# Constant products on TensorE between the squares of an RWKV-7 kernel's first chunk

## The chip, the cores and the metric

The kernel runs on one core of one Trainium2 chip. The metric is the device time of one execution in microseconds (us); three runs of the kernel before gave 713.66, 718.1 and 712.8, so the median is 713.66 us. The profile is one execution recorded by the hardware profiler. The engines are TensorE (PE, with its weight loads as PEld), VectorE (DVE), ScalarE (ACT) and GpSimd (POOL); SyncE (SP) issues most transfers, each engine has its own queue of instructions, and works through it in order.

## The reference

The kernel computes a linear-attention recurrence and then an MLP, all in 32-bit floats. For each of 4 x 8 batch and head pairs, over 768 steps, with a state of 40 x 40:

```
for t in range(S):
    y[:, :, t] = einsum('bhd,bhde->bhe', rt, state)
    Sa = einsum('bhde,bhe->bhd', state, at)
    state = state * wt[:, :, None, :] - einsum('bhd,bhe->bhde', Sa, bt)
    state = state + einsum('bhd,bhe->bhde', vt, kt)
x = y.transpose(0, 2, 1, 3).reshape(B * S, H * D)      # 3072 x 320
h = x @ w_in                                           # 320 x 2048, given as 64-bit floats
out = (0.5 * h * (1 + erf(h / sqrt(2)))) @ w_out       # 2048 x 320, given as 64-bit floats
```

## The kernel before

The 768 steps are cut into 12 chunks of 64. Within a chunk the recurrence is written as matrices. N (a against scaled b), A (a against scaled k), RV (r against v) and M are products of 64 x 64 blocks, masked to their strict upper triangle by VectorE (`masked`, line 575). The chunk needs the inverse of a triangular matrix made from N. Its 32 x 32 diagonal blocks are inverted first; `corner` and `joined` put the 64 x 64 inverse Tt together from them. Then follow sa and saT, M, and QY, which gives the chunk's output rows and its next state; `outputs` scales these. The MLP of a chunk is cut into pieces, and `fill` puts them between the steps of later chunks.

Chunks after the first have their 32 x 32 blocks inverted on GpSimd, column by column (`start_inverse`, lines 672 and 674), and the result goes through memory (`store_inverse`, `fetch_inverse`). The first chunk does it on TensorE (`squares`, line 712): in five rounds the power of N is squared and the inverse T is updated. A round is 64 small products, then a copy of the power by ScalarE (line 736), a transpose by VectorE (line 737) and, but for the first round, an addition to T by VectorE (line 739). The next round waits for all of these. `squares` is a generator: each `next(zero)` in the main part runs one round, and the first one only the preparation. `corner_direct` and `joined_direct` (products J and J2) then build Tt of the first chunk, with copies by ScalarE and VectorE.

Meanwhile the weights, which come as 64-bit floats, are converted by integer and float steps on VectorE, ScalarE and POOL (`to_float`, lines 319 to 333); `convert(n)` starts n such conversions and finishes those that it finds half done, and `first_load` and `second_load` bring the raw words.

The order of the work is written out by hand: `manual_schedule` keeps the instructions of each engine in the order in which the program calls for them. Waits follow from data and from buffers. All results of TensorE go to one pool of four buffers, `duo`, each of 2 x 512 columns and 128 partitions. Two helpers issue products whose result nothing uses: `warm(columns, ...)` takes a buffer of its own and multiplies the identity with a broadcast of the constant `cum_m`, one product for each argument, of 128 columns for each unit; `keep(n)` asks that the next `duo` begins with one such product of n x 128 columns, in the buffer that it hands out. Before the change `warm` is not called after its definition.

`make_y2(0)` takes the two buffers of QY. For the first chunk there is no earlier state, so it issues nothing else.

Of the kernel before, what the change touches and what calls it, by code (L numbers as in the profile page):

```python
# [19 lines left out]
def kernel(  # L20
# [71 lines left out]
    def keep(columns):  # L92

        asked[:] = [columns]

    def duo(name):
        pt = psum.tile([P, 2, 512], FP32, tag="duo", name=name)
        while asked:
            n = asked.pop()
            mm(pt[:, 0, :n * P], ident, cum_m.unsqueeze(1).to_broadcast([P, n, P]))  # L100
        return pt

    def half(j, n=HP):
        return slice(j * HP, j * HP + n)
# [4 lines left out]
    def mm(o, lhsT, rhs, first=True):  # L109
        nc.tensor.matmul(o, lhsT, rhs, start=first, stop=True, skip_group_check=True)  # L110
# [39 lines left out]
    def rows(t):  # L150
        return t[:, :G * DM].rearrange("p (g h d) -> p g h d", g=G, h=H)
# [142 lines left out]
    def flat(t):  # L294
        return t.rearrange("p j g n t -> p (j g n) t")
# [42 lines left out]
    def convert(n, last=False):  # L338

        for _ in range(n):  # L340
            begun.append(queue.pop(0))
            next(begun[-1], None)
            if len(begun) > 1:
                next(begun.pop(0), None)
        if last:
            while begun:
                next(begun.pop(0), None)
# [62 lines left out]
    def first_pieces(kts, part, eng):  # L410
        queue.extend(first_convert(kt, part, eng) for kt in kts)
# [4 lines left out]
    def run(steps):  # L416
        for _ in steps:
            pass
# [4 lines left out]
    def logs(c):  # L423
        logw = raws[c, "w"][:, :G * DM]
        nc.scalar.activation(logw, logw, ACT.Ln)
# [66 lines left out]
    def scale_k(c, eng=nc.gpsimd):  # L492
        rwv, _ = decays[c]
        ks = turned_in[c]["ks"] = padded[:, 2 + c % 2] if c < NB else k_rows[c % 2]
        to = ks[:, :, :, :D] if c < NB else rows(ks)
        eng.tensor_tensor(to, raws.pop((c, "k")), rwv, ALU.mult)
# [35 lines left out]
    def turn_k(c):  # L532
        t = turned_in[c]
        if c >= NB:
            kT = by_batch(side("k_turned", "conv", 2))
            turn(kT, c, "k_turned")
            en = t.pop("en")
            nc.vector.tensor_tensor(en, kT, en, ALU.mult)
            t["kT"] = parts_by_batch(en)
            return  # L540
        kT = side("kT", "kT", 1)
        nc.scalar.copy(kT, flip(by_pair(t["ks"]), "kT_ps"))
        t["kT"] = parts(kT)
# [15 lines left out]
    def turn_r(c):  # L559
        rT = side("rT", "rT", 2)  # L560
        if c < NT:
            raw = raws.pop((c, "r"))
            nc.scalar.copy(rT, flip(lambda q, m: raw[:, NP * q + m].rearrange("p g d -> p (g d)"), "rT_ps"))
        else:
            turn(rT.rearrange("p q m (e t) -> p (q m e) t", e=2), c, "r")
        turned_in[c]["rT"] = parts(rT)
# [7 lines left out]
    def masked(to, pt):  # L574
        nc.vector.tensor_tensor(to, pt, upper.unsqueeze(1).to_broadcast([P, 2 * G * NP, C]), ALU.mult)  # L575

    def products(name, lT, rT, swap):

        pt = duo(name).rearrange("p j (g n t) -> p j g n t", g=G, n=NP)
        for g in range(G):  # L580
            for n in range(NP):
                for e in range(2):
                    for j in range(2):
                        mm(pt[half(e ^ j if swap else e), j, g, n], lT[half(j, D), g, n, e],
                           rT[half(j, D), g, n, e])
        return flat(pt)
# [32 lines left out]
    def make_RV(c, mask=True):  # L619
        t = turned_in[c]  # L620
        t["RV_ps"] = products("RV_ps", t["vT"], t["rT"], False)
        if mask:
            mask_RV(c)

    def mask_RV(c):
        t = turned_in[c]
        masked(flat(t["VR"])[:, :, D:], t.pop("RV_ps"))
# [12 lines left out]
    def make_av(c):  # L640
        t = turned_in[c]
        av = duo("av")[:, :, :G * NP * D].rearrange("p x (g i d) -> p x g i d", g=G, i=NP)
        for g, i, x, e, q, m in units():
            mm(av[half(e ^ x), x, g, i], t["A"][half(e), x, g, i], t["VR"][half(e), g, q, m, :D])
        avs = t["avs"] = avs_ring()
        nc.scalar.copy(avs[:, :, :DM], av.rearrange("p x g i d -> p x (g i d)"))
# [65 lines left out]
    def squares(c, turned, Z, ZT, eng):  # L712

        N = flat(turned_in[c]["N"])
        turned = turned.rearrange("p (n t) -> p n t", n=NBL)
        both = Z.rearrange("p (n x t) -> p n x t", n=NBL, x=2)
        ZT = ZT.rearrange("p (n t) -> p n t", n=NBL)
        power, T = both[:, :, 0], both[:, :, 1]
        nc.vector.transpose(turned, N)
        for rows, cols in quads:  # L720
            eng.tensor_tensor(T[rows], N[rows, :, cols], ident[rows, rows].unsqueeze(1).to_broadcast([BL, NBL, BL]),
                              ALU.add)
        yield
        for k in range(5):
            last = k == 4
            pt = duo("sq").rearrange("p z (n t) -> p (z n) t", t=2 * BL)
            for n in range(NBL):
                for rows, cols in quads:
                    if k == 0:
                        mm(pt[rows, n, :BL], turned[rows, n, cols], N[rows, n, cols])  # L730
                    elif last:
                        mm(pt[rows, n, BL:], ZT[rows, n], T[rows, n])
                    else:
                        mm(pt[rows, n], ZT[rows, n], both[rows, n].rearrange("p x t -> p (x t)"))
            if not last:
                nc.scalar.copy(power, pt[:, :, :BL])
                nc.vector.transpose(ZT, pt[:, :, :BL])
            if k:
                nc.vector.tensor_tensor(T, T, pt[:, :, BL:], ALU.add)
            yield  # L740
        nc.vector.transpose(ZT, T)
        inverses[c] = T, ZT, power

    def corner_direct(c, engs):
        T, L, Js = inverses[c]
        N = flat(turned_in[c]["N"])
        Tt = inverses[c] = Tt_ring()
        turned_in[c]["blocks"] = T, Js
        J = duo("J").rearrange("p z (n t) -> p z n t", n=NBL)
        for n in range(NBL):  # L750
            for q in range(2):
                mm(J[hi[q], q, n], N[lo[q], n, BL:], L[lo[q], n])
        for q in range(2):
            nc.scalar.copy(Js[hi[q]], J[hi[q], q])
        for (rows, cols), eng in zip(quads, engs):
            copy = eng.copy if eng is nc.scalar else eng.tensor_copy
            copy(flat(Tt)[rows, :, cols], T[rows])
# [88 lines left out]
    def make_M(c):  # L846
        t = turned_in[c]
        masked(flat(t["SM"])[:, :, D:], products("M_ps", t["saT"], t["rT"], False))

    def make_y2(c):  # L850


        t = turned_in[c]
        t["QY"] = [duo("QY")[:, :, :NP * VC].rearrange("p e (i c) -> p e i c", i=NP) for g in range(G)]
        if state[0] is None:
            return
        tn = state[0][1]
        for i in range(NP):
            for e in range(2):
                for x in range(2):  # L860
                    for g in range(G):
                        mm(t["QY"][g][half(x), e, i, D:], tn[half(g, D), e, i, half(x)],
                           t["rT"][half(g, D), i // NA, 2 * (i % NA) + x, e], i == 0)
# [189 lines left out]
    def warm(*columns):  # L1053

        pt = duo("warm")
        for n, cols in enumerate(columns):
            mm(pt[:, n % 2, :cols * P], ident, cum_m.unsqueeze(1).to_broadcast([P, cols, P]))
# [16 lines left out]
    scale_a(0)  # L1074
    make_N(0)
    zero = squares(0, spare_w, *spare_N, nc.gpsimd)
    next(zero)
    sums(1)
# [18 lines left out]
    mask_A(0)  # L1097
    turn_r(0)
    next(zero)
    next(zero)  # L1100
    make_RV(0, False)
    run(zero)
    scale_k(1, nc.vector)
    corner_direct(0, (nc.scalar, nc.scalar, nc.scalar, nc.scalar))
    first_load(False, 1, eng=nc.sync)
    make_av(0)
    make_y2(0)
    turn_k(1)
    make_X(0)
    first_pieces((1, 2), 0, nc.gpsimd)  # L1110
    mask_RV(0)
    first_pieces((3,), 0, nc.vector)
    load_VR(1)
    joined_direct(0)
# [9 lines left out]
    make_saT(0)  # L1124
    convert(0, True)
    convert(1)
    make_M(0)
    logs(2)
    keep(1)
    make_QY(0)  # L1130
    first_load(False, 2, early(5, 4), eng=nc.sync)
    convert(1)
# [235 lines left out]
```

## Time and profile before

| what | value |
|---|---|
| median of three runs | 713.66 us |
| span of the profiled execution | 709.1 us |
| median less that span | 4.6 us |
| TensorE busy | 669.7 us, 94% of the span |
| VectorE busy | 365.5 us, 52% |
| ScalarE busy | 222.3 us, 31% |
| POOL busy | 350.2 us, 49% |
| mean granted clock of TensorE | 0.958 |

The profiled execution's own time is its span and some 4.6 us around it, if it was an execution like the median one. The page also gives the busy share in 40 slices of the span, some 17.7 us each, in tenths, and under them the clock that TensorE was granted, where 9 stands for 90% or more of full speed. The same numbers can be asked for any window. The timeline lists instructions in order with their start, their duration, and in brackets the idle time before them with what ended it. In it a 32-bit product of TensorE shows as two records.

### The profile page before, as it was taken

The numbers are of one execution on the slowest core, as the hardware profiler recorded it, in microseconds if no ns is written. First come the engines' busy times: TensorE is split into PE (matmuls) and PEld (weight loads), VectorE is DVE, ScalarE is ACT, GpSimd is POOL, SyncE is SP. The second block draws the span as 40 slices with busy tenths as digits, with TensorE's granted clock in tenths as the row PEclk, the third lists the DMA queues.
The fourth block names the chain that finished last, engine by engine and source line by source line (L and its number), as shares of the span: only waits on it lengthen the run. The fifth ranks groups of instructions, "written<-read, shape, count | busy, mean of one in ns | idle before, by whom it ended". The sixth has DMA issues, their size and how long they took to land.

```text
span 709.1 us, 32732 instructions
## 1 busy us (share of the span) xinstructions
PE 669.7 (94%) x14778; PEld 587.1 (83%) x14778; DVE 365.5 (52%) x481; ACT 222.3 (31%) x308; POOL 350.2 (49%) x798
## 2 busy tenths in 40 slices
PE   7578897879999999999999999999999999999997
PEld 4567786757877877899899898998998898998987
DVE  2334689993354365375484483573671772522303
ACT  5124674444140240351241332232323413112020
POOL 5284458810851851861862853845836827800000
PEclk9775798999999999999999999999999999999999
DMA  9689538864667647656656747657648646020100
GB/s 130 121 167 151 104 87 203 136 128 88 123 122 113 132 94 110 133 100 113 124 102 121 137 87 128 125 93 128 133 84 144 130 86 85 20 55 4 31 8 19
DMA packets 287923, 74.46 MB, mean 105 GB/s; under 512 B 265736, under 2 KB 284456, under 8 KB 287784
## 3 DMA queue, kind: packets, MB, share of 16 engines
q1 hardware_dynamic: 283360, 68.20, 52.6%
q0 software_dynamic: 864, 2.36, 2.2%
q8 instruction: 116, 1.90, 1.2%
q10 hardware_dynamic: 3560, 1.80, 1.0%
q14 instruction: 23, 0.19, 0.1%
HBM read 58.69 MB, written 9.70 MB: 96 GB/s over the span
## 4 chain that ended last, share of the span: by engine, by line
PE 81%; DVE 6%; DMA 3%; ACT 3%; SPq 3%; issue 2%; ACTq 1%; DVEq 0%
PE ph L993 26%; PE po L946 19%; PE po L1010 7%; PE QY L110 6%; PE J L110 2%; PE av L110 2%; PE A_ps L110 2%; PE X L110 2%; PE sq L110 2%; PE RV_ps L110 2%; DMA a_pairs<-in_a_dram 2%; PE sap L110 2%; PE saT_ps L110 2%; PE M_ps L110 2%; PE wT_ps L110 1%
## 5 line engine op out<-in xcount | busy, mean ns | idle before, releaser
L993 PE MATMUL ph<-xt,w_in_sb 64*128 64x256 f32 x1920 | 219.4, 381 | 0.0
L672 POOL TENSOR_TENSOR tmp<-W,Nb 128x126 f32<-128x126 f32 (+22 forms) x310 | 124.3, 401 | 160.0 <-DMA Nb<-N 137.0
L993 PEld LDWEIGHTS ph<-xt,w_in_sb 64*128 64x128 f32 x1920 | 182.4, 187 | 22.1 <-issue 0.3
L674 POOL TENSOR_TENSOR W<-W,tmp 128x126 f32<-128x126 f32 (+22 forms) x310 | 132.4, 427 | 24.3
L995 ACT ACTIVATE gt<-ph 128x1024 f32<-128x1024 f32 x48 | 49.1, 1024 | 152.5 <-PE ph L993 152.3
L946 PE MATMUL po<-w_out_sb,gt 128*128 128x160 f32 x576 | 83.0, 302 | 0.1
L946 PEld LDWEIGHTS po<-w_out_sb,gt 128*128 128x128 f32 x576 | 78.7, 190 | 2.2 <-DVE gt L966 0.4
L1010 PE MATMUL po<-w_out_sb,gt 128*128 128x320 f32 x192 | 55.8, 448 | 1.1 <-ACT wpT L443 1.1
L1010 PEld LDWEIGHTS po<-w_out_sb,gt 128*128 128x128 f32 x192 | 36.7, 195 | 16.7 <-issue 1.5
L186 DVE STREAM_TRANSPOSE aT<-a_pairs 128x1024 f32<-128x1024 f32 x9 | 11.2, 1247 | 46.6 <-DMA a_pairs<-in_a_dram 46.6
L802 DVE COPY Tt<-J 32x512 f32<-32x512 f32 x9 | 6.2, 689 | 54.5 <-ACT Tt L802 54.5
L786 ACT COPY Js<-J 128x256 f32<-128x256 f32 x11 | 4.1, 370 | 94.6 <-PE J L110 94.6
L998 DVE TENSOR_TENSOR half<-gt 128x1024 f32<-128x1024 f32 x9 | 11.4, 1271 | 29.6 <-ACT gt L995 29.6
L946 PE MATMUL po<-extra,half 128*128 128x160 f32 x176 | 26.1, 303 | 0.0
L320 ACT ACTIVATE conv<-conv,rebias 128x320 uint32<-128x320 uint32 (+1 forms) x26 | 16.1, 624 | 29.0 <-DVE conv L319 23.1
L575 DVE TENSOR_TENSOR SM<-M_ps,upper 128x1024 f32<-128x1024 f32 x12 | 14.5, 1207 | 19.7 <-PE M_ps L110 19.7
L946 PEld LDWEIGHTS po<-extra,half 128*128 128x128 f32 x176 | 24.2, 190 | 0.3
L995 ACT ACT_TABLE_LOAD x10 | 12.8, 1283 | 36.0 <-PE ph L993 36.0
L950 DVE TENSOR_TENSOR os<-os,po 128x160 f32<-128x160 f32 x36 | 11.5, 319 | 23.6 <-PE po L946 17.9
L946 PE MATMUL po<-extra,gt 128*128 128x160 f32 x144 | 21.0, 299 | 0.0
L662 POOL MEMSET W<- 128x512 f32 x10 | 5.3, 528 | 31.5 <-DMA inv<-W 31.5
L886 DVE TENSOR_TENSOR xt<-QY,wpT 128x512 f32<-128x512 f32 x24 | 15.4, 684 | 10.2 <-PE QY L110 9.6
(224 smaller groups left out, 1134.7 us busy)
## 6 DMA issues: line engine op xcount, KB each, us to landing
Nb<-N SPq DMA_DIRECT2D x20, 256.0 KB
VR<-in_v_dram SPq DMA_DIRECT2D x24, 160.0 KB
out_dram<-os SPq DMA_DIRECT2D x48, 80.0 KB
b_rows<-in_b_dram SPq DMA_DIRECT2D x22, 160.0 KB
k_rows<-in_k_dram SPq DMA_DIRECT2D x22, 160.0 KB
N<-N SPq DMA_DIRECT2D x44, 64.0 KB
Tt<-inv SPq DMA_DIRECT2D x44, 64.0 KB
a_pairs<-in_a_dram SPq DMA_DIRECT2D x18, 144.0 KB
```

The source lines that it names most:

```text
L110: nc.tensor.matmul(o, lhsT, rhs, start=first, stop=True, skip_group_check=True)
L320: nc.scalar.activation(power, power, ACT.Relu, bias=rebias, scale=8.0)
L575: nc.vector.tensor_tensor(to, pt, upper.unsqueeze(1).to_broadcast([P, 2 * G * NP, C]), ALU.mult)
L672: eng.tensor_tensor(t, W[:, :rows, j:j + 1].to_broadcast([P, rows, rest]), Nb[:, j:j + 1, j + 1:].to_broadcast([P, rows, rest]), ALU.mult)
L674: eng.tensor_tensor(W[:, :rows, j + 1:], W[:, :rows, j + 1:], t, ALU.add)
L886: nc.vector.tensor_tensor(xt[:, :NP, g * P:(g + 1) * P].rearrange("p i (e t) -> p i e t", e=2), Y, wp[:, g, :, :, :C], ALU.mult)
L946: nc.tensor.matmul(po[:, n, :DM // 2], l_[:, f], r_[:, f], start=f == 0, stop=f == NF // 2 - 1)
L950: nc.vector.tensor_tensor(to, one_, other, ALU.add)
L993: nc.tensor.matmul(ph[:, x, s], w_in_sb[half(x), kt, p * P:(p + 1) * P], xt[half(x), kt], start=kt == 0, stop=kt == NK - 1)
L995: nc.scalar.activation(gt[:, 4 * q:4 * q + 4].rearrange("p (x s) t -> p x s t", x=2), ph, ACT.Gelu)
L998: nc.vector.tensor_tensor(s1, block(1, 0), block(1, 1), ALU.add)
L1010: nc.tensor.matmul(po[:, g], gt[:, f, g * P:(g + 1) * P], w_out_sb[:, f], start=f == 0, stop=f == NF - 1)
```

## The change

Eight calls of `warm` are put in. Five stand at the head of the five rounds of squares, with 2, 3, 4, 2 and 2 products of 512 columns. One with 3 follows the last round, one with 2 stands in front of `make_M(0)` and one with 2 in front of `make_QY(0)`. RV is multiplied between the last two rounds instead of after the last, and its mask follows the last round at once. `make_y2(0)` goes from behind `make_av(0)` to just in front of `make_QY(0)`, and the `keep(1)` there, whose product goes in front of the next result, vT of chunk 1, is dropped.

```
         for k in range(5):
             last = k == 4
+            warm(*(4,) * (2, 3, 4, 2, 2)[k])
             pt = duo("sq").rearrange("p z (n t) -> p (z n) t", t=2 * BL)
...
     next(zero)
+    make_RV(0, False)
     next(zero)
-    make_RV(0, False)
     run(zero)
+    mask_RV(0)
+    warm(4, 4, 4)
     scale_k(1, nc.vector)
     corner_direct(0, (nc.scalar, nc.scalar, nc.scalar, nc.scalar))
     first_load(False, 1, eng=nc.sync)
     make_av(0)
-    make_y2(0)
     turn_k(1)
     make_X(0)
     first_pieces((1, 2), 0, nc.gpsimd)
-    mask_RV(0)
     first_pieces((3,), 0, nc.vector)
...
     convert(1)
+    warm(4, 4)
     make_M(0)
     logs(2)
-    keep(1)
+    warm(4, 4)
+    make_y2(0)
     make_QY(0)
```

On TensorE the order after the change is: N of chunk 1, 2 constant products, round 1, 3 products, round 2, 4 products, round 3, kT, A, vT, rT, 2 products, round 4, RV, 2 products, round 5, 3 products, J, av, kT of chunk 1, J2, A of chunk 1, sa, saT, 2 products, M, 2 products, QY. On VectorE the mask of RV stands ahead of the scaling of chunk 1's k instead of behind it. The queues of ScalarE, POOL and SP keep their order.

More of the change, by code (lines that the diff above doesn't have):

```diff
@@ L725, in squares @@
             last = k == 4
+            warm(*(4,) * (2, 3, 4, 2, 2)[k])
             pt = duo("sq").rearrange("p z (n t) -> p (z n) t", t=2 * BL)
@@ L1099 @@
     next(zero)
+    make_RV(0, False)
     next(zero)
-    make_RV(0, False)
     run(zero)
+    mask_RV(0)
+    warm(4, 4, 4)
     scale_k(1, nc.vector)
@@ L1106 @@
     make_av(0)
-    make_y2(0)
     turn_k(1)
@@ L1110 @@
     first_pieces((1, 2), 0, nc.gpsimd)
-    mask_RV(0)
     first_pieces((3,), 0, nc.vector)
@@ L1126 @@
     convert(1)
+    warm(4, 4)
     make_M(0)
     logs(2)
-    keep(1)
+    warm(4, 4)
+    make_y2(0)
     make_QY(0)
```

## The prediction

> **What bounds the kernel now.** I read the page's forty slices first (17.7 us each), because what the change adds is work for TensorE.
>
> ```profile
> span 709.1 us, 32732 instructions
> ...
> PE   7578897879999999999999999999999999999997
> ...
> PEclk9775798999999999999999999999999999999999
> ```
>
> From slice 10 (160 us) to the end TensorE is full at full clock, so time won or lost at the start is kept only if it still stands there. All edits lie in slices 2 to 5, where TensorE is neither full nor fast. The next view is the table of windows. In windows of one us from 20 to 95 us the clock changed only near 25.5, 32.3, 35.8, 39.2, 49.4 and 80.1 us, always a multiple of 3.4 us apart; so I cut the windows there.
>
> ```profile
> 22.10:25.50 3.40, 2.01 (x111) 1.61 (x110) 0.94 (x2) 1.01 (x1) 1.54 (x1) 1.00 0.59 85
> 25.50:28.90 3.40, 1.39 (x85) 1.25 (x84) 1.00 (x2) 0.58 (x1) 0.77 (x3) 0.51 0.39 61
> 28.90:32.30 3.40, 2.97 (x113) 3.00 (x117) 0.28 (x1) 0.00 (x0) 0.00 (x0) 0.50 0.26 52
> 32.30:35.80 3.50, 1.33 (x89) 1.20 (x82) 1.29 (x2) 0.58 (x1) 0.00 (x0) 0.99 0.89 236
> 35.80:39.20 3.40, 3.40 (x87) 3.23 (x77) 0.68 (x2) 0.59 (x1) 2.56 (x10) 0.50 1.13 215
> 39.20:42.60 3.40, 2.30 (x83) 1.99 (x83) 1.35 (x3) 1.01 (x1) 2.77 (x9) 1.00 0.55 128
> ...
> 46.00:49.40 3.40, 1.23 (x104) 1.07 (x92) 1.29 (x2) 0.58 (x1) 2.93 (x7) 1.00 1.23 203
> 49.40:52.80 3.40, 2.98 (x138) 2.63 (x128) 1.62 (x3) 0.00 (x0) 2.85 (x8) 0.51 0.81 114
> ...
> 76.70:80.10 3.40, 3.40 (x81) 3.15 (x73) 1.37 (x4) 0.70 (x2) 2.55 (x2) 0.50 1.06 213
> ```
>
> The first number after the length is TensorE's busy time; the third from the end is its clock. Windows with 1.23 and 1.33 us of work were followed by half clock. After 46.0 to 49.4 it stays at 0.50 for nine windows, to 80.1; windows busy for 2.98 us of small products did not bring it back. The chain of waits says that TensorE is on the path there (squares, J, av, A_ps, sap, M_ps, QY), with Scalar and Vector steps between. These Vector steps I read from the timeline:
>
> ```profile
> 63.13 0.69 DVE L768 COPY Tt<-J 32x512 f32<-32x512 f32 x1 [7.72 <-ACT Tt L768]
> ...
> 67.19 0.82 DVE L831 COPY SM<-sap 128x640 f32<-128x640 f32 x1
> 67.94 1.21 DVE L575 TENSOR_TENSOR A<-A_ps,upper 128x1024 f32<-128x1024 f32 x1
> ...
> 71.50 0.69 DVE L324 SCALAR_TENSOR_TENSOR conv<-w_out_sb,conv 128x512 uint32<-128x512 uint32 x1 [1.68 <-ACT conv L320]
> 72.92 1.23 DVE L575 TENSOR_TENSOR SM<-M_ps,upper 128x1024 f32<-128x1024 f32 x1 [0.73 <-PE M_ps L110]
> 74.06 1.50 DVE L319 TENSOR_SCALAR conv<-w_out_sb 128x512 uint32<-128x512 uint32 x1
> ...
> 81.74 0.70 DVE L772 STREAM_TRANSPOSE L<-Tt 128x512 f32<-128x512 f32 x1
> ```
>
> VectorE is nearly closed from 63.1 to 69.8: a faster TensorE cannot pull that stretch forward.
>
> **The price of one product.** Eight 320-column products of the MLP (16 records) take 4.50 us at full clock, so 512 columns cost 4.50 / 8 x 512 / 320 = 0.90 us, and 1.8 at half. The 20 added are 18.0 us of TensorE at full clock. None waits for anything not long done, so each starts as TensorE comes free; what exceeds the old wait delays the next square.
>
> **The squares, step by step, at full clock.** A 64-column square costs 2.0 us at full clock (1.99 at 44.65) against 3.43 at half (29.33); a 32-column one 1.7 (43 records in 0.57).
> - N_ps of chunk 1 ends at 24.77, unchanged. Two products 1.8, first square 1.7: end 28.3 (before 27.82, with half clock and a 1.14 us gap called issue). I let the long products hide that gap; its bounds are 0 and 1.14.
> - Three products 2.7 in a wait of 1.5, square 2.0: 33.0 (32.80).
> - Four, 3.6, in a wait of 2.1, square 2.0: 38.6 (37.81).
> - kT now 1.06 instead of 1.74, ScalarE's copy 1.01, A_ps 1.16, vT 1.9, rT 1.0: 44.9 (44.72).
> - Two, 1.8, where there was no wait at all, square 2.0: 48.7 (46.70).
> - RV 1.16, at no cost: it lies in the 2.1 us that the last square waits for Scalar and Vector, and the copy of rT that it needs ended at 45.77. Two products 1.8 more end after that wait; last square 1.7: 53.4 (51.08).
> - Three, 2.7, against 1.5 us of Vector; J 1.04 instead of 1.92, and RV's 3.1 us (51.0 to 54.1) no longer ahead of it: **57.1 (55.96)**.
>
> So J ends 1.1 us later, although nothing runs at half clock. RV's mask (1.22) now goes ahead of the scaling of k (0.78) on VectorE. It ends near 56.8, before kT of chunk 1 wants it at 58.3; if that cover went, it would cost up to 1.2.
>
> **From J to chunk 1.** ScalarE then copies without a break: 4.46 us for Js, Tt and av, 1.01 for kT, 0.57 for Tt. Before, 1.0 us of waits for TensorE lay between. The 1.1 and the 1.0 cancel: VectorE's copy of Tt ends at 63.95 (63.82), and its closed stretch at 69.9. TensorE's part is early: sap and saT end at 66.2 (69.75), so ScalarE's conversion no longer queues behind saT's copies; the 1.68 us idle at 71.50 shrinks to 0.4, and the mask of M (whose 2 products and M itself end by 69.2) ends at 72.3 (74.15), 1.9 early. QY takes 3.0 instead of 5.83: 75.4 (80.02). Its two products lie under the mask. Taking QY's buffers later moves no instruction, as the first chunk has none there; dropping the 128-column product saves 0.3 behind QY.
>
> What is late next is L of chunk 1. Its buffer comes free with POOL's second conversion, 80.20 before. That follows ScalarE's and VectorE's conversions. The 1.50 us of L319 (0.42 elsewhere) ended just after POOL's first conversion, so I let it follow POOL: 74.5 (75.56), 1.1 early, and POOL's second ends at 79.1. L then starts at 79.1 (81.74): **2.6 early**. Bounds: 1.1, if only POOL's shift counts, to 4.6, QY's shift. L's data, stored and fetched through SP's queue, do not shift (issued to 72.9); that landing is not shown, and I take it to be before 79.
>
> TensorE waits from 77 to 80 for it, a window as thin as the ones that fell. Then J and a keep product run at half until 83.5; that returns 0 to 1.0 us, and I take 0.6. **Sum: 2.0 us less.** From there to 112 us the chain is Scalar and Vector work in order, which moves as a whole; transfers have room (DMA share 0.2 to 0.5 from 84 to 112). The profiled span of 709.1 becomes 707.1; the median of 713.66 lies 4.6 above the span, and I add that: 711.7.
>
> **A rule against the change.** Clock rows first: half clock from 35.8 follows a window whose longest wait is 2.17 us. The Trainium skill, "TensorE: Matmul & The Clock Gate", section "HAM oscillation — how this bites in real kernels", asks only that no idle gap exceed about 3.4 us. By it alone the filled waits were harmless, and the change is its 1.1 us at J: 714.8. The trace disagrees with it; I go by the rows.
>
> **Rivals.**
> 1. Overfilled waits, slower: products where there was 0 to 2.1 us of wait cost more than the clock returns. Place: the window from 25.5 and the one from 42.6. If half clock still holds in both (the windows before them are not full: 2.3 us busy with the kT wait), 1.7 us are lost in each, and J ends 4.5 late. It decides once J is more than 3.7 late, for then L is not early. With a fallen clock at 80: 1.0 + 0.8 = about 2 slower, 715.7. For it: 2.01 us busy was followed by half clock at 25.5. Against: dense products replace the small ones, and 2.30 held at 39.2.
> 2. Hidden anyway: J's delay and the closed Vector stretch eat the gain, or a later dip (the clock fell to 0.50 for 116 to 120) moves the other way: 713.7, within 1.
> 3. L isn't held by POOL: all of QY's 4.6 comes through, 709.1.
>
> **How the numbers follow.** Forecast (1 to 4 us less) 0.5, rival 1 0.2, rival 2 0.18, rival 3 0.12. The range runs from 706.5 (rival 3 and a lucky later window of 2.6) to 717.0 (rival 1 with 1.3 more of half clock). Within 1%, 7.1 us, is about what a measurement of this kernel can tell from no change; nearly all lies there. Beyond, either way, takes something that no row shows: 0.06 each.
>
> **What would show it.** Clock 1.00 from 25.5 to about 63; J ending near 57; the Vector copy of Tt unmoved near 64; M's mask 2 early; L near 79. The forecast is wrong if L319 keeps its time whatever POOL does, if half clock returns between the squares, or if the chain after 112 us does not move with L.

## The result and the profile after

The kernel after takes 718.82 us (median of nine runs, 717.06 to 722.65), the kernel before 714.0 us (nine runs on the same chip, 711.18 to 718.1). The ratio is 1.0068, with a 95% interval of 1.0043 to 1.0094: slower by some 4.8 us, where 2.0 us less was forecast. The profiled execution of the kernel after has a span of 717.1 us and a mean granted clock of 0.979 (0.958 before). That run took 718.82 us, so 1.7 us lie around the span.

The page of the kernel after: its span, TensorE's busy time with the number of its matrix instructions, the 40 slices (17.9 us each) of TensorE and of its clock, and the queue that brings the instructions.

```profile
span 717.1 us, 32807 instructions
...
PE 680.9 (95%) x14816; PEld 584.5 (82%) x14816; DVE 365.9 (51%) x481; ACT 222.2 (31%) x308; POOL 348.0 (49%) x798
...
PE   7898897869999999999999999999999999999997
...
PEclk8799999989999999999999999999999999999999
...
q8 instruction: 116, 1.90, 1.2%
```

The clock did what was hoped. In slices 3 to 5 it reads 9 throughout, where the kernel before had 7, 5 and 7, and the digits of TensorE are as high or higher in slices 2 to 5. Over 24.5 to 82.0 us the mean clock rose from 0.64 to 0.88 and TensorE's busy time from 44.27 to 49.86 us. The time is longer nevertheless. The last line, which the prediction did not use, matters below: 116 packets with 1.90 MB of instructions, 16 KB each.

The table of windows of the kernel after, cut as before (the first number after the length is TensorE's busy time, the third from the end its clock).

```profile
22.10:25.50 3.40, 1.48 (x24) 1.28 (x28) 1.75 (x2) 1.01 (x1) 1.54 (x1) 0.83 0.50 86
25.50:28.90 3.40, 3.40 (x63) 2.25 (x56) 1.23 (x1) 0.00 (x0) 0.00 (x0) 0.50 0.00 0
...
35.80:39.20 3.40, 3.40 (x94) 2.11 (x83) 1.29 (x2) 0.58 (x1) 1.81 (x7) 1.00 1.06 227
...
49.40:52.80 3.40, 3.40 (x160) 2.48 (x162) 0.00 (x0) 0.69 (x2) 2.91 (x7) 1.00 1.17 147
52.80:56.20 3.40, 1.72 (x49) 1.44 (x42) 1.29 (x2) 0.32 (x1) 2.85 (x8) 0.83 0.54 86
56.20:59.60 3.40, 3.40 (x69) 1.31 (x67) 0.00 (x0) 0.00 (x0) 2.84 (x8) 0.66 0.95 137
```

The half clock from 35.8 and the long one from 49.4 are gone. The one from 25.5 stayed, and a new, shorter one begins in the window from 52.8 and goes on into the next. That window is busy for only 1.72 us, although no engine kept TensorE waiting in it. The timeline of TensorE in the kernel after shows why (start, duration, operation; in brackets the idle time before it, and what ended it).

```profile
27.00 3.78 PE L110 MATMUL warm<-cum_m,ident 128*128 128x512 f32 x4
30.71 1.61 PE L110 MATMUL sq<-N,st 32*32 32x32 f32 x128
...
50.42 1.99 PE L110 MATMUL sq<-Nb,W 32*32 32x64 f32 x128
52.34 0.79 PE L110 MATMUL RV_ps<-rT,vT 40*64 40x64 f32 x34
54.81 0.94 PE L110 MATMUL RV_ps<-rT,vT 40*64 40x64 f32 x30 [1.68 <-issue]
55.68 3.36 PE L110 MATMUL warm<-cum_m,ident 128*128 128x512 f32 x4
58.97 1.43 PE L110 MATMUL sq<-Nb,W 32*32 32x32 f32 x128
...
63.10 1.20 PE L110 MATMUL J<-W,N 32*32 32x32 f32 x64
...
78.77 1.23 PE L110 MATMUL M_ps<-rT,saT 40*64 40x64 f32 x64
```

After 34 records of RV, TensorE stands still for 1.68 us with "issue" as the reason, which means that nothing the profile shows held it. The clock falls, and the two products behind it take 3.36 us instead of 1.8. In front of the first square the two products take 3.78 us, since the clock was half there too. ScalarE begins to copy J at 64.40 us (56.06 before), and VectorE follows:

```profile
70.26 0.69 DVE L769 COPY Tt<-J 32x512 f32<-32x512 f32 x1 [6.26 <-ACT Tt L769]
...
80.06 1.23 DVE L575 TENSOR_TENSOR SM<-M_ps,upper 128x1024 f32<-128x1024 f32 x1 [2.04 <-PE M_ps L110]
81.20 0.42 DVE L319 TENSOR_SCALAR conv<-w_out_sb 128x512 uint32<-128x512 uint32 x1
...
86.82 0.70 DVE L773 STREAM_TRANSPOSE L<-Tt 128x512 f32<-128x512 f32 x1
```

That is VectorE's timeline of the kernel after. The copy of Tt begins 7.1 us later than before (63.13), the mask of M 7.1 (72.92), L of chunk 1 5.1 (81.74). From there to the end of the span it is 630.3 us, 627.4 in the first profile of before and 630.1 in a second one that is told of below.

### The profile page after: what moved, and what is told of

Same layout as the page of the kernel before. It is cut to its first block, busy times and chain, and to the rows that moved or that the text cites. A ratio compares the mean times of both kernels' runs of the same rounds, so it can differ in the third digit from the quotient of the medians.

```text
span 717.1 us, 32807 instructions
## 1 busy us (share of the span) xinstructions
PE 680.9 (95%) x14816; PEld 584.5 (82%) x14816; DVE 365.9 (51%) x481; ACT 222.2 (31%) x308; POOL 348.0 (49%) x798
## 4 chain that ended last, share of the span: by engine, by line
PE 77%; DVE 3%; SPq 2%; ACT 2%; issue 1%; DMA 1%; ACTq 1%; DVEq 0%
PE ph L994 29%; PE po L947 19%; PE po L1011 7%; PE QY L110 6%; PE J L110 2%; PE X L110 2%; PE av L110 1%; PE sap L110 1%; PE saT_ps L110 1%; PE A_ps L110 1%; PE RV_ps L110 1%; PE M_ps L110 1%; PE N_ps L110 1%; SPq L898 1%; PE wT_ps L110 1%
## 5 line engine op out<-in xcount | busy, mean ns | idle before, releaser
L672 POOL TENSOR_TENSOR tmp<-W,Nb 128x126 f32<-128x126 f32 (+22 forms) x310 | 121.3, 391 | 159.4 <-DMA Nb<-N 136.4
L1011 PEld LDWEIGHTS po<-w_out_sb,gt 128*128 128x128 f32 x192 | 37.0, 197 | 18.1 <-ACT wpT L443 2.5
L186 DVE STREAM_TRANSPOSE aT<-a_pairs 128x1024 f32<-128x1024 f32 x9 | 11.2, 1246 | 42.3 <-DMA a_pairs<-in_a_dram 42.3
L951 DVE TENSOR_TENSOR os<-os,po 128x160 f32<-128x160 f32 x36 | 11.5, 319 | 28.9 <-PE po L947 23.2
L320 ACT ACTIVATE conv<-conv,rebias 128x320 uint32<-128x320 uint32 (+1 forms) x26 | 16.1, 623 | 29.7 <-DVE conv L319 23.3
L110 PE MATMUL warm<-cum_m,ident 128*128 128x512 f32 x40 | 23.8, 736 | 0.0
L662 POOL MEMSET W<- 128x512 f32 x10 | 5.3, 529 | 35.8 <-DMA inv<-W 35.8
```

Source lines behind the costliest of these rows:

```text
L186: nc.vector.transpose(to.rearrange("p n (s y) -> p n y s", y=2), raws.pop((c, n)).rearrange("p n (y d) -> p n y d", y=2)[:, :, :, :BL])
L320: nc.scalar.activation(power, power, ACT.Relu, bias=rebias, scale=8.0)
L672: eng.tensor_tensor(t, W[:, :rows, j:j + 1].to_broadcast([P, rows, rest]), Nb[:, j:j + 1, j + 1:].to_broadcast([P, rows, rest]), ALU.mult)
L951: nc.vector.tensor_tensor(to, one_, other, ALU.add)
L1011: nc.tensor.matmul(po[:, g], gt[:, f, g * P:(g + 1) * P], w_out_sb[:, f], start=f == 0, stop=f == NF - 1)
```

## The experiments

In what follows N is the end of chunk 1's N on TensorE, J the start of ScalarE's first copy of J, L the start of VectorE's first transposes for L. One profile is one execution, and such landmarks move: the kernel before, profiled a second time, has J at 59.26 instead of 56.06. The verdicts therefore rest on the timed ratios, and the profiles on what recurs in several.

Several theories were tried against each other, and the expectations name them by letters or by what they say. The overfilled waits are theory A: only TensorE's time counts, and a product delays the next step by what it exceeds the wait. Theory B puts the time on the new order or on QY's late buffers. Another let the loads on SP's queue hold something up. Theory F, which came last, says that TensorE also has to be fed: its instructions arrive in packets of 256, which is 128 matrix records with their 128 weight loads, and small products use these up faster than the next packet comes.

### Order, squares and tail apart

`e1_order_only` is the kernel after without any of the 20 products: the new order alone.

```
-            warm(*(4,) * (2, 3, 4, 2, 2)[k])
...
-    warm(4, 4, 4)
...
-    warm(4, 4)
     make_M(0)
     logs(2)
-    warm(4, 4)
```

> The changed kernel without any of its 20 products: RV between the last two rounds, its mask early, QY's buffers late, the keep product gone. Theory A (the products are longer than the waits that they fill): the slowdown goes; RV's 3.1 us no longer stand between the last square and J, so J ends 1 to 3 us earlier than before and the time is 711 to 714. Theory B (the new order or QY's late buffers cost the time): at least 3 of the 4.8 us stay, 717 or more.

Measured: 716.41 us against 715.22; ratio 1.0017, interval 0.9983 to 1.0051. The new order costs or brings nothing that can be told from zero, so theory B's 717 us or more did not come; the 711 to 714 us that theory A gave didn't either. In its one profile (an execution of 720.62 us) TensorE stands still with "issue" for 3.08 us in RV, which now follows the fourth square, and for 2.94 us in the fifth square: in that execution what the order was to save went there.

`e2_squares_only` is the kernel before with the products of the rounds alone.

```
         for k in range(5):
             last = k == 4
+            warm(*(4,) * (2, 3, 4, 2, 2)[k])
```

> The kernel before with only the 13 products at the heads of the five rounds; RV, its mask, QY's buffers and the keep product as before. Theory A: 13 products of 0.9 us are 11.7 at full clock, and the waits of the rounds hold 1.5 + 2.1 + 2.1 of them, so J ends 6 to 9 us late, and with half clock for some of the products more; part of it comes back by full clock after J: 716 to 721. Theory B: within 1 us of before, 713 to 715.

Measured: 724.17 us, ratio 1.0109 (1.0074 to 1.0145). The products of the rounds are slower by themselves, and seem to cost more than the whole change (1.0068), though the two intervals overlap.

`e3_tail_only` is the kernel after without that line; the three products behind the rounds, those in front of M and QY, and the order stay.

> The changed kernel without the 13 products of the rounds, but with the new order and with the 3 + 2 + 2 products behind the last round and in front of M and QY. Theory A: J ends at most 2 us later than before (2.7 of products in a wait of 1.5, RV no longer there), and the 3 us that the changed kernel won between J and L of chunk 1 stay: 709 to 713. Theory B: 717 or more. Third theory (without products in the rounds the clock falls before J and what follows J wins nothing): 713 to 716.

Measured: 719.44 us, ratio 1.0049 (1.0015 to 1.0082). That is slower where theory A gave 709 to 713 us, though only three of its products stand between N and J; its profile is of a quick execution (716.0 us), and what makes its median long stays open. The parts don't add up (1.0109 and 1.0049 against 1.0068 for both): the one gives back a part of what the other costs.

`without_M_QY` tries one part. It is the kernel after without the four products in front of M and QY.

```
-    warm(4, 4)
     make_M(0)
     logs(2)
-    warm(4, 4)
     make_y2(0)
```

> The changed kernel without the four products in front of M and QY. In its profile M's products started 2.4 us after the last copy of saT (76.37 to 78.77) because two products at half clock stood before it, and QY 0.5 after its mask. Theory A: M's mask ends 1.5 to 2.5 us earlier after J, L 1.5 to 2.5 earlier, time 716 to 717.5. If full clock for QY is what these four buy: QY takes 5 us instead of 3.2, the two cancel, 718 to 719.5.

Measured: 721.59 us against 714.93; ratio 1.0098 (1.0063 to 1.0132). Its timeline of TensorE has M and QY at half clock again:

```profile
77.67 2.46 PE L110 MATMUL M_ps<-rT,saT 40*64 40x64 f32 x64 [0.69 <-ACT saT L843]
81.46 3.05 PE L110 MATMUL QY<-SM,extra 64*64 64x104 f32 x64 [1.33 <-DVE SM L575]
```

From J to L it takes 24.7 us, the two profiles of the kernel before 25.7 and 24.0, and three of the kernel after 22.4, 22.6 and 22.2. Over all runs, eight profiles without these four products have 23.3 to 25.7 us and eight with them 21.3 to 23.2; `e4_fit`, told of next, has two of the four and 25.8. So the four products in front of M and QY return some 2.5 us from J to L, and the loss lies between N and J. The timed ratios agree in sign, but their intervals overlap.

### Fewer and more products

`e4_fit` sizes the products to the waits of the kernel before: 0, 1, 2, 0 and 1 in the rounds, 1 behind them, 1 in front of M and 1 in front of QY.

```
-            warm(*(4,) * (2, 3, 4, 2, 2)[k])
+            warm(*((), (4,), (4, 4), (), (4,))[k]) if k in (1, 2, 4) else None
...
-    warm(4, 4, 4)
+    warm(4)
...
-    warm(4, 4)
+    warm(4)
     make_M(0)
     logs(2)
-    warm(4, 4)
+    warm(4)
```

> The changed kernel with fewer products, sized to the waits at full clock: none, 1, 2, none and 1 at the heads of the rounds, 1 behind the last, 1 in front of M and 1 in front of QY, 7 instead of 20. Theory A: no wait is overfilled by more than 0.3 us at full clock, so J ends at 54 to 57, the win after J stays, 707 to 711. Theory B: 717 or more. If the clock cannot be held with 7 products: 711 to 715.

Measured: 716.83 us, ratio 1.001 (0.9976 to 1.0044): like the kernel before. The 707 to 711 us of theory A did not come.

`no_wait_places` leaves out the products of rounds 1 and 4, where the kernel before had no wait.

```
-            warm(*(4,) * (2, 3, 4, 2, 2)[k])
+            if k in (1, 2, 4):
+                warm(*(4,) * (2, 3, 4, 2, 2)[k])
```

> The changed kernel without the two products of round 1 and the two of round 4, the places where the square had no wait at all; 16 products stay. Theory A (products beyond a wait are paid in full): J ends 3 to 4 us earlier after N than with all 20 (33 to 34.5 us instead of 37.3), and the time is 714 to 716. Theory F (the packets set the pace, and the products lie under their lateness): the gaps come back where the products were, J moves by less than 1.5 us, the time stays at 717 to 719.

Measured: 717.6 us, ratio 1.0036 (1.0005 to 1.0068). That is about half the loss, as far as overlapping intervals tell.

`two_waits_only` is the kernel before with one product in the wait of round 2 and two in that of round 3.

```
+            if k in (1, 2):
+                warm(*(4,) * k)
```

> The kernel before with three products alone: one of 0.9 us in the 1.5 us wait of round 2, two of 1.8 in the 2.1 us wait of round 3; nothing else moves. Theory A: none is beyond its wait, the squares of rounds 2 and 3 run at full clock and save up to 2.3 us: 712.5 to 715. Theory F or a full clock that is worth nothing here: kT, the packets and ScalarE's copies take the gain back, 714.5 to 717.

Measured: 716.06 us, ratio 1.002 (0.9993 to 1.0047). Even products that fit a real wait bring nothing that can be told from zero.

`double_dose` is the kernel after with 4, 6, 8, 4 and 4 products in the rounds, 13 more, which are 11.7 us of TensorE at 0.90 each.

> The changed kernel with twice the products in the rounds: 4, 6, 8, 4 and 4, that is 13 more, 11.7 us at full clock. Theory A (the waits are already overfilled): every added product delays J in full, J ends 10 to 13 us later than 64.4 less the 2 to 3 us of half clock that denser work avoids, and the time is 727 to 731. Theory F (packets set the time; products only lie under their lateness): part of the added time hides the packets, J ends 5 to 8 later, 722 to 726.

Measured: 722.33 us against 715.28; ratio 1.0121 (1.0076 to 1.0166). Its profile (an execution of 728.15 us, the slowest of four) has the clock at 1.00 from 7.1 to 75.3 us:

```profile
7.10:75.30 68.20, 59.23 (x1489) 39.26 (x1488) 18.33 (x22) 21.08 (x27) 31.47 (x76) 1.00 0.84 138
```

Its timeline of TensorE has a stop before J, and another behind it:

```profile
67.44 0.25 PE L110 MATMUL J<-W,N 32*32 32x32 f32 x3 [0.28 <-issue]
...
72.15 0.37 PE L110 MATMUL J<-Nb 32*32 32x32 f32 x11 [1.41 <-issue]
```

Here the aim of the change is fully met, and the kernel is slower still. But 11.7 us more of products lengthened N to J by only 4.5 us and the time by some 3.5: something else was hidden under them. That is in the range of theory F and not in that of theory A.

### Where the time between N and J goes

The timelines of TensorE, added up from N to J: constant products, waits for another engine (the bracket names one), stops with "issue", and the rest, which is the useful products.

| run | N to J | products | waits | issue | rest |
|---|---|---|---|---|---|
| before | 31.3 | 0 | 7.0 | 2.4 | 21.9 |
| before_again | 35.0 | 0 | 7.0 | 4.7 | 23.4 |
| after | 37.3 | 18.0 | 1.1 | 1.7 | 16.6 |
| after_again | 40.7 | 16.5 | 1.1 | 5.0 | 18.0 |
| after_control | 38.9 | 18.4 | 1.1 | 2.2 | 17.1 |
| double_dose | 43.5 | 26.0 | 1.1 | 0.3 | 16.1 |
| e1_order_only | 38.1 | 0 | 6.4 | 8.4 | 23.2 |
| e2_squares_only | 39.0 | 12.1 | 1.4 | 5.4 | 20.1 |
| e3_tail_only | 36.7 | 4.1 | 4.8 | 5.8 | 22.0 |
| e4_fit | 36.2 | 7.8 | 1.4 | 5.8 | 21.2 |
| no_wait_places | 37.8 | 14.7 | 1.1 | 4.3 | 17.7 |
| without_M_QY | 39.4 | 14.8 | 1.1 | 4.3 | 19.2 |
| two_waits_only | 32.5 | 4.0 | 3.5 | 3.4 | 21.5 |
| quiet_before | 33.7 | 0 | 7.0 | 5.0 | 21.8 |
| quiet_after | 38.7 | 14.8 | 1.1 | 4.7 | 18.1 |
| dense_products | 49.6 | 16.3 | 1.1 | 11.2 | 21.1 |
| before_small | 38.0 | 1.6 | 4.8 | 7.6 | 24.1 |

Means of the two profiles of before and the three of after: the products cost 17.6 us; they bring back 5.9 of waits, 5.4 in the useful products by the faster clock, and 0.6 of stops. That leaves 5.8 us lost from N to J (33.2 to 38.9; the parts are rounded). With the 2.5 us returned from J to L the loss is 3.3 us, less than the timed 4.8. These parts are rough: the four profiles without products between N and J have 31.3 to 38.1 us (mean 34.5), the five with all sixteen 37.3 to 40.7 (mean 39.0), which makes the loss there 4.5 us. Where the rest of the timed 4.8 lies the profiles don't show. L itself is 4.9 later in these profiles, because N, ahead of every edit, was 1.5 later in them, by chance as far as the runs show (24.1 to 27.1 over all of them, with no tie to the edits).

`before_again` and `after_again` are second profiles of the two kernels, with one time each.

> The kernel before, unchanged, profiled a second time. In all traces so far TensorE stands still at every 128th small product (records 984, 1112, 1239 of its stream) and goes on 1.3 to 1.7 us after a 16 KB packet of the instruction queue has landed. Theory F (the time of the first chunk is set by how late these packets come, which changes from execution to execution): the gaps before records 984, 1112 and 1239 differ from the first profile's 0.41, 0.84 and 0.66 us by 1 to 3 us in sum, J ends at 57 to 62 instead of 55.96, the span is 711 to 716. Theory A alone (only the products matter): J ends within 1 us of 55.96 and the span within 2 of 709.1.

> The changed kernel, unchanged, profiled a second time. Its first profile began the edited stretch late (N of chunk 1 ended at 27.07, not 24.2 to 25.8 as in the eight other traces) and with half clock. If that was one execution's bad luck: N ends at 24.2 to 25.8, J 36 to 38 us after it (37.3 in the first profile), so at 60 to 63, L 22 to 23 us after J, span 713 to 718. If the products themselves cause it: N ends at 27 and J at 64 again.

Measured: 715.14 us with a span of 713.4, and 720.43 us with a span of 718.7. So 1.7 us lie around a span, and the first profile of the kernel before was a quick execution. The timeline of TensorE in `before_again`:

```profile
25.75 1.39 PE L110 MATMUL sq<-N,st 32*32 32x32 f32 x85 [0.74 <-issue]
...
51.99 1.18 PE L110 MATMUL sq<-Nb,W 32*32 32x32 f32 x72 [2.01 <-issue]
53.10 1.77 PE L110 MATMUL RV_ps<-rT,vT 40*64 40x64 f32 x56
56.82 0.49 PE L110 MATMUL RV_ps<-rT,vT 40*64 40x64 f32 x8 [1.94 <-issue]
57.24 1.92 PE L110 MATMUL J<-W,N 32*32 32x32 f32 x64
```

In the first profile of the kernel before:

```profile
26.41 1.39 PE L110 MATMUL sq<-N,st 32*32 32x32 f32 x85 [1.14 <-issue]
...
49.90 1.19 PE L110 MATMUL sq<-Nb,W 32*32 32x32 f32 x72 [0.41 <-issue]
...
53.62 0.49 PE L110 MATMUL RV_ps<-rT,vT 40*64 40x64 f32 x8 [0.84 <-issue]
```

The stops stand at the same places of the program in both: in front of the last 85 records of the first square, the last 72 of the fifth, the last 8 of RV. Only their length changes. Counted through the stream of matrix records they are 128 apart, give or take two (in the first profile records 984, 1112, 1239, 1366 and 1494), and when an edit adds records they shift by just as many: RV stops after 56 records in the kernel before, after 34 in the kernel after (22 more records; the fifth square's 128, one packet's worth, stand behind RV there), after 50 in `e4_fit` (6 more), after 30 in `e2_squares_only` (26 more). The trace of the instruction queue gives the other half. Some of the stops, in us:

| run, stopping in | TensorE stops | packet of 16 KB under way | TensorE goes on |
|---|---|---|---|
| before, fifth square | 49.49 | 47.16 to 48.49 | 49.90 |
| before, RV | 52.78 | 51.28 to 52.34 | 53.62 |
| before, av | 57.62 | 55.65 to 56.76 | 58.27 |
| after, RV | 53.13 | 51.83 to 53.28 | 54.81 |
| dense_products, fourth square | 50.59 | 50.62 to 52.02 | 53.51 |
| dense_products, RV | 56.18 | 54.97 to 56.17 | 58.06 |
| dense_products, small products | 60.61 | 59.90 to 61.19 | 62.62 |
| dense_products, fifth square | 64.55 | 64.81 to 65.86 | 67.26 |
| before_small, third square | 36.07 | 37.96 to 39.22 | 40.78 |

TensorE goes on 1.3 to 1.9 us after a packet has landed, each time. The table is a choice, but the rest agrees: the 17 profiles have 49 stops over 0.25 us with "issue" from N to J. Every one stands within four records of a multiple of 128, counted from record 984, and ends 1.2 to 1.9 us after a packet has landed. And the next packet starts only 1.1 to 5.7 us after TensorE has gone on. TensorE uses up 128 small records in some 2 us at full clock, and the packets come less often than that.

### Loads moved away

Whether the loads on SP's queue delay the packets was tried in both kernels: chunk 1's r is loaded later, and the third group of raw weights too.

```
     joined_direct(0)
-    load_r(1)
...
     make_QY(0)
-    first_load(False, 2, early(5, 4), eng=nc.sync)
...
     fetch(2, "k", k, nc.sync)
+    load_r(1)
     fetch_inverse(1)
+    first_load(False, 2, early(5, 4), eng=nc.sync)
```

> The kernel before, with two groups of loads of SP issued later: the r rows of chunk 1 (4 transfers) behind the load of chunk 2's k, and the third quarter of the first weight's words (6 transfers) behind the fetch of chunk 1's inverse. No work is left out. Theory F with data transfers delaying the instruction packets: from 48 to 62 us the packets start 1.0 to 2.0 us after TensorE passes a boundary, not up to 5.7; the gaps there sum to under 2.5 us, J ends at 55 to 57, and the time is 709 to 713 against some 715 before. If the packets' lateness does not depend on these transfers: gaps as before, time 714 to 717.

> The changed kernel with the same two groups of loads issued later. Theory F with data transfers delaying the packets: the gaps of 1.7, 1.8 us in RV and saT shrink to under 0.7, no half clock follows them, J ends 2 to 4 us earlier than 64.4, the time is 713 to 717. Theory A (overfilled waits): J moves by less than 1.5 us and the time stays at 717 to 720.

Measured: `quiet_before` 719.66 us, ratio 1.0066 (1.0035 to 1.0098); `quiet_after` 725.31 us, ratio 1.0149 (1.0116 to 1.0182). The moved loads cost some 4 to 5 us, at least in part later on (from L to the end 633.9 us in `quiet_before`, 627.4 and 630.1 in the kernel before), and the stops stayed: 2.24 and 2.74 us from N to J in `quiet_before`, 1.10, 2.47 and 1.16 in `quiet_after`. Nothing here ties the late packets to these two groups of loads. What makes one packet start 1.1 us and another 5.7 us after TensorE has gone on is open.

### The number of products, at equal TensorE time

The packets were tested by themselves. `dense_products` is the kernel after with the two long products of rounds 4 and 5 replaced by 64 products of 32 columns: 128 records instead of 4, and about as much TensorE time.

```
+    def small():
+        pt = duo("small").rearrange("p z (n t) -> p (z n) t", t=2 * BL)
+        for n in range(NBL):
+            for rows, cols in quads:
+                mm(pt[rows, n, :BL], ident[rows, rows], cum_m[rows, :BL])
...
-            warm(*(4,) * (2, 3, 4, 2, 2)[k])
+            small() if k > 2 else warm(*(4,) * (2, 3, 4)[k])
```

> The changed kernel with the two long products of round 4 and the two of round 5 each replaced by 64 products of 32 columns. Their TensorE time stays: 1.7 us at full clock against 1.8; their records are 128 instead of 4, so two more packets of instructions. Theory A: J ends within 1 us of the changed kernel's (37 to 41 us after N), the time is 718 to 720. Theory F: each added packet takes 3.6 to 6 us where the product took 1.8, J ends 4 to 8 us later, the time is 722 to 727.

Measured: 729.61 us, ratio 1.0221 (1.0168 to 1.0274) to the kernel before. Beside it, timed on the same chip, stands the kernel after as a control.

> The changed kernel once more, timed beside the next two on the same chip and profiled a third time: 1.004 to 1.010 of the kernel before (1.0068 so far), J 37 to 41 us after N of chunk 1.

Measured: 720.6 us against 716.05; ratio 1.0068 (1.0035 to 1.0102), as the first time. So the same time of products, cut into more instructions, costs 9.0 us. The timeline of TensorE in `dense_products`:

```profile
53.51 1.50 PE L110 MATMUL sq<-Nb,W 32*32 32x64 f32 x90 [2.93 <-issue]
54.94 1.25 PE L110 MATMUL RV_ps<-rT,vT 40*64 40x64 f32 x38
58.06 1.01 PE L110 MATMUL RV_ps<-rT,vT 40*64 40x64 f32 x26 [1.88 <-issue]
59.01 1.60 PE L110 MATMUL small<-cum_m,ident 32*32 32x32 f32 x102
62.62 0.58 PE L110 MATMUL small<-cum_m,ident 32*32 32x32 f32 x26 [2.01 <-issue]
62.97 1.58 PE L110 MATMUL sq<-Nb,W 32*32 32x32 f32 x102
67.26 0.63 PE L110 MATMUL sq<-Nb,W 32*32 32x32 f32 x26 [2.71 <-issue]
```

Between two stops lie 90 + 38, 26 + 102 and 26 + 102 records, 128 each time, and TensorE goes on 4.55, 4.56 and 4.64 us apart. Nothing else has a part in that stretch: no bracket names an engine. Stops grew from 2.2 to 11.2 us against the control; the rest grew by 4.0, at a lower clock (0.76 from N to J instead of 0.86; whether the stops alone or also the small products as such lowered it is not separated); the products were 2.1 shorter. Together that is the 10.8 by which N to J grew.

`before_small` is the kernel before with one such group of 64 at the head of round 3, where it has a wait of 2.17 us and the group takes 1.55.

```
+            if k == 2:
+                small()
```

> The kernel before with 64 products of 32 columns put into the wait of round 3: 1.7 us at full clock in a wait of 2.1 us. Theory A: they lie within the wait and J does not move by more than 0.5 us but for the clock, 714 to 716. Theory F: one more packet in the stretch, J 2 to 4 us later (33 to 39 us after N instead of 31 to 35), 716.5 to 719.

Measured: 720.43 us, ratio 1.0068 (1.0039 to 1.0097), 4.4 us slower. Its timeline of TensorE:

```profile
32.85 0.62 PE L110 MATMUL small<-cum_m,ident 32*32 32x32 f32 x43
34.29 0.93 PE L110 MATMUL small<-cum_m,ident 32*32 32x32 f32 x85 [0.82 <-issue]
35.25 0.83 PE L110 MATMUL sq<-Nb,W 32*32 32x64 f32 x42
40.78 2.56 PE L110 MATMUL sq<-Nb,W 32*32 32x64 f32 x86 [4.70 <-issue]
```

The products fit into the wait: the third square begins at 35.25, 9.7 us after N, and in the kernel before at 34.93, 10.2 after N. By TensorE's time alone that is free. What is added lies 42 records into the square: 4.70 us for a packet that lands at 39.22. Nor is it the buffer that the group takes: `two_waits_only` takes one at the same place, with 4 records in it instead of 128, at a ratio of 1.002. The timed ratio carries this; the length of one stop in one profile would not. Theory A falls with these two runs. F gave the right order for both, and its numbers were somewhat low.

No version that was run beats the kernel before.

## Why the prediction was wrong

**The step that failed is "The squares, step by step, at full clock".** It gave 32.3 us from N to J (24.77 to 57.1), and 38.9 was the mean of three profiles. Split as in the table, the step holds 14.4 us of products (16 at 0.90), the 1.1 us wait for kT, and 16.8 of useful products; the profiles have 17.6, 1.1, 17.2, and 3.0 of stops. So the waits and the useful products were as forecast. Two terms were not:
- The stops, 3.0 us. "I let the long products hide that gap; its bounds are 0 and 1.14": this took one stop for the whole matter, and asked neither why it was there nor where the next would be. The profile that it worked from had two more, of 0.41 and 0.84 us, and the sum takes all 2.4 us as gone. Long products do hide stops near them (`double_dose`: 0.3 us), but in the kernel after one is left in RV in all three profiles (1.68, 1.37 and 2.25 us), where RV follows a square without a pause.
- The products, 3.2 us more than forecast, nearly all of it half clock. "At full clock" was an assumption for the first two products, which took 3.78 us in two of the profiles, and for the two of round 5, which took 3.36 and 3.78 us in two of them behind the stop in RV. In the third a stop of 1.98 us in the fifth square did the same to the three products behind it (4.54 us). The price of a product itself was right: 1.88 to 1.98 for two, 2.84 for three and 3.70 for four at full clock.

**The base.** "The median of 713.66 lies 4.6 above the span, and I add that": only 1.7 us lie around a span. The other 2.9 was the quickness of the execution that was profiled, and 31.3 us from N to J was the lower of two values (35.0).

**The squares' gain was worth less than the clock suggested.** From N to J there are about 890 small records in the kernel before, 6.9 packets of 128. The pace seen from stop to stop is 3.72 us for 128 records (before, 49.90 to 53.62, clock 0.50), 4.6 (`dense_products`, clock 0.50 for most of it) and 4.71 (`double_dose`, 67.44 to 72.15, clock 1.00), and no bracket in these stretches names an engine. An estimate from it of what the 6.9 packets take is 26 to 33 us. The kernel before took 31.3 and 35.0 with more than half of that at half clock. There was less to win than a doubled clock promises, and this explains why the small doses that cost little (`e4_fit`, `two_waits_only`) bring nothing. That last inference is argued from the pace, which is that of single executions, and not shown by itself.

**From J to L** 22.0 us was forecast, and 22.4 measured, against 24.9 as the mean of before. This part held in size: QY took 3.1 us (to 84.93) instead of 5.83. Its reasons held in part. L319 took 0.42 us behind the mask of M instead of 1.50; POOL's conversion had ended at 81.10, just before it began, which neither speaks against its tie to POOL nor tests it. L came 0.5 us after POOL's second conversion had ended (86.28), right behind the scaling of the state on VectorE, so that here POOL was not what it waited for last. And the two products in front of M ended at 78.6, behind the wait that they were to fill, since saT's copies ended at 76.4: they took 3.44 us behind one more stop with "issue", of 1.83 us, in saT; the mask of M waited 2.04 us for that.

**The rivals.** Rival 1, the overfilled waits, named the right sign, the window from 25.5 as one place, and a price of 1.7 us for products at half clock (2.0 and 1.6 measured in the profile after). Its other place, from 42.6, ran at 1.00; half clock met the products of round 5 instead. Its point of decision, J more than 3.7 late, was passed too: 5.8 by the mean lengths from N. It still gave too little, 715.7: it had no term for the stops, and the range, up to 717.0, was built from it. Rivals 2 and 3 didn't occur. The time lies outside the range and within the 1% that was given the most weight.

**The rule on the clock.** The Trainium skill, "TensorE: Matmul & The Clock Gate", section "HAM oscillation — how this bites in real kernels", asks that no idle gap exceed about 3.4 us. The runs disagree as the rows of before did: the half clock near 56 us followed a longest gap of 1.68 us. What brings the clock back the rows do not settle: of windows at half clock in the kernel before, 28.9 to 32.3 (2.97 us busy) was followed by 0.99, 49.4 to 52.8 (2.98) and 59.6 to 63.0 (3.40) by 0.50. Going by the rows was right, but the clock was not what decided.

**A rule that the prediction left out.** The Trainium skill, "Runtime: NRT & Kernel Launch", section "Instruction fetch mechanics", says that an engine's instructions are refilled in blocks of 16 KiB, 256 instructions, and: "The cost of crossing a 16 KiB boundary is one DMA tail-bump, mostly hidden." The trace agrees on the size (116 packets for 1.90 MB). On "mostly hidden" the runs agree for most of the kernel (from 130 us on, the stops over 0.25 us add up to 0.4 us in the first profile of before and 1.3 in that of after) and disagree for small products: single crossings cost 0.3 to 4.7 us, and 11.2 us in all from N to J in `dense_products`.

**Shown and open.** Shown: the order alone does nothing measurable, the products of the rounds cost more than they bring back (`e2_squares_only`), those in front of M and QY bring some back (in the profiles; the timed ratios do not separate it), and the number of products costs time at equal TensorE time. That packets are what TensorE stands still for rests on the trace (128 records between stops, going on 1.2 to 1.9 us after a landing) and on the two runs that changed the number of records. Why one packet starts later than another is open, and so is where the part of the timed 4.8 us lies that the profiles' 3.3 or less leaves over, and why `e3_tail_only` is slow.

## What to carry to other kernels

In a stretch of small products, count TensorE's instructions as well as its time: here 128 records took some 3.7 to 4.7 us from stop to stop, at clocks of 0.50 and of 1.00, and stops with "issue" in the profile that stand a multiple of 128 records apart are the sign. A constant product in a wait is paid for with whatever it exceeds the wait, at the clock that it meets, and a higher granted clock is no gain by itself (1.00 from 7.1 to 75.3 us in `double_dose`, and 1.2% slower). Profile the kernel before twice before the landmarks of one execution are used as a base: here J moved by 3.2 us with no change at all.

## What the runs showed of the hardware

The instruction packets were not expected to be on the path. Each took 0.9 to 1.6 us, and in stretches of small products TensorE stopped for it for 0.3 to 4.7 us; a stop lowered the clock as a wait does, so it was paid for twice (the 1.68 us in RV, and then 3.36 us for products of 1.8). The packets were not fetched far ahead: after each of the 49 stops the next one started only once TensorE had gone on, 1.1 us later at the earliest. The lengths of these stops differ between executions of the same kernel at the same places (0.41 and 2.01 us in front of the last 72 records of the fifth square before), which makes them a likely source of the scatter in the times of the kernel before, 710 to 726 us over all its runs.
